# One fused attention, gated-convolution and mixer kernel: weights decoded two tiles to an operation, pooled scores by head, a new order of work

## The chip, the cores and the metric

The kernel runs on one core of one Trainium2 chip. The metric is the device time of one execution in microseconds (us). The engines are named as the profile names them: PE (TensorE) multiplies and PEld loads its weights, DVE is VectorE, ACT is ScalarE, POOL is GpSimd, SP issues the transfers.

## The reference

Three blocks follow one another. Sizes: batch 4, 8 heads, 576 positions, head width 64, so 4 x 576 tokens of 512 channels.

```python
# 1: attention, scale 1/8, factor 4
q_d, k_d, v_d = (t.reshape(B, H, 144, 4, 64).mean(axis=3) for t in (q, k, v))
out = np.repeat(softmax(scale * q_d @ k_d.T) @ v_d, 4, axis=2)          # pooled
out += softmax(where(abs(i - j) < 4, scale * q @ k.T, -1e9)) @ v        # local
x = out.transpose(0, 2, 1, 3).reshape(B, 576, 512)
# 2: gated convolution, w_in 512 x 1024, three taps over the positions, w_out 1024 x 512
h = relu(x @ w_in)
x = (h * sigmoid(conv(h, conv_w))) @ w_out
# 3: low-rank mixing of the positions (rank 32), then a channel product, 512 -> 2048 -> 512
u = x + (x.T @ U @ V).T
out = u + relu(u @ w_ch1) @ w_ch2
```

Inputs q, k and v are 32-bit; the weights of blocks 2 and 3 are 64-bit numbers and reach the chip as pairs of 32-bit words.

## The kernel before

**Attention** works on 16 pairs (two heads of one batch on 128 partitions). Pair p needs three loads: `lq` (q and k, 576 KB), `lw` (values for the local part, 384 KB), `lr` (values for the pooled part, 288 KB). `qs` sums q and k over four positions (`sums`, L355); `qd` copies the summed q of both heads into a zeroed block matrix (`q_blocks`, L374). `S`, `Sd` are the local and pooled scores on PE, `M`, `Md` the maxima, `D` subtracts them on DVE (`dp` does it on PE), `E`, `Ed` are the exponentials on ACT, `R`, `re`, `r` row sums and reciprocals, `n`, `nd` the normalisation, `T`, `Td` transposes, `c`, `cd` copies out of PSUM, `V`, `Vd` products with the values, `xd`, `x` the sum into the tile `X`, which holds two batches. `vs` sums the pooled values. A suffix says the engine: `nv`, `ndv`, `vsv`, `cv`, `cdv`, `xdv`, `wO`, `gL`, `pL`, `mL`, `sA`, `sl`, `bl` run on DVE; `n`, `nd`, `vs`, `wo`, `gl`, `pl`, `ml`, `sa`, `sL`, `bL` on POOL; `c`, `cd`, `xd` on ACT. `f.n` puts n matmuls into PE's queue whose results nobody uses.

**Weights** come in tiles of 128 x 512 64-bit words (512 KB by the profile). `wl` loads a tile; `wd` decodes it to a 32-bit number: step 0 on ACT (L583), steps 1 to 3 on DVE (L585, L587, L590). `wh` copies the rounded upper part on ACT (L603), `wo` or `wO` takes the remainder on POOL or DVE (L606). Every product of blocks 2 and 3 is made of three matmuls, high x high, high x low, low x high. Decoded values wait in three buffers `wval` of one tile each. There are 16 such tiles for block 2 and 32 for block 3.

**Block 2** runs over 6 token blocks of 384 and, in each, over 8 blocks f of 128 hidden channels; n = 8 * block + f. `1.n.cc` is the first product (L719), `r1` the relu, `c0` and `c1` the taps, `th` tanh, `gt`/`gm` the gate, `gh` and `gl`/`gL` its upper part and remainder, `2.n.c` the second product (L773). Token block 0 needs pairs 0 to 3 in `X`, token block 1 (from `1.8.0` on) pairs 4 to 7 too, and with block 0 all 16 tiles have been needed.

**Block 3**: `mh`, `mi`, `mo`, `ma` mix; then the channel product by a scheme with 7 instead of 8 half products (`p`, L925; second product `4`, L957). Its left operands `as` are made from decoded tiles (`sa`, `sh`, `sl`), written to HBM (`sw`) and read again twice (`sr`) into 10 buffers.

**Order**: nothing is reordered by a compiler. The string `SEQ` is a list of some 2,900 words; each word calls one function, and each engine executes its instructions in the order of the list. An instruction waits for its data and for its buffer, and what stands behind it on its engine waits with it. All loads are issued by SP in the order of the list; `load` makes the 44 first ones also wait for an earlier load, so that about 900 KB are under way.

Of the kernel before, what the change touches and what calls it, by code (L numbers as in the profile page):

```python
# [1064 lines left out]
```

## Time and profile before

| | us |
|---|---|
| runs | 725.91, 726.84, 728.79 (median 726.84) |
| the profiled execution's own time | 723.91 |
| its span, first to last instruction | 722.1 |
| busy in the span: PE, DVE, ACT, POOL | 696.3, 463.2, 354.7, 186.0 |
| mean granted PE clock | 0.988 of full |

Busy PE includes matmuls that overlap: the group of L957 shows 216.9 us for 864 matmuls of 393 ns each, so two lie over one another most of the time. Shares over the span mix stages with different limits; the text that follows goes by stages.

### The profile page before, as it was taken

Reading aid. Unit: us, or ns where it says so; the run is one execution under the profiler, and the core shown is the slowest. Engines: PE = TensorE matmul, PEld = TensorE weight load, DVE = VectorE, ACT = ScalarE, POOL = GpSimd, SP = SyncE. Lnnn points to the kernel's source line nnn. Section 1 sums busy time; section 2 is a strip of 40 time slices with the busy share of each in tenths; the row PEclk is TensorE's granted clock in tenths of the full one; section 3 lists DMA queues with packets and bytes.
Section 4 is the critical chain, followed back from the end, with each engine's and each line's share of the span. In section 5 each row is a group of like instructions: output and inputs, shape, how many; then the busy total and the mean of one; then the engine's idle time right before and its main releaser. Section 6 shows DMA issues by size and latency. Waiting matters only on the chain.

```text
span 722.1 us, 14566 instructions
## 1 busy us (share of the span) xinstructions
PE 696.3 (96%) x5785; PEld 615.8 (85%) x5785; DVE 463.2 (64%) x807; ACT 354.7 (49%) x818; POOL 186.0 (26%) x186
## 2 busy tenths in 40 slices
...
GB/s 265 285 303 246 179 99 24 73 73 75 61 2 1 1 1 30 87 162 134 302 170 237 226 244 228 159 182 119 129 118 117 96 101 199 117 131 118 114 45 88
DMA packets 40580, 96.43 MB, mean 134 GB/s; under 512 B 4672, under 2 KB 5184, under 8 KB 40512
## 3 DMA queue, kind: packets, MB, share of 16 engines
...
q8 instruction: 46, 0.75, 0.4%
...
## 4 chain that ended last, share of the span: by engine, by line
PE 82%; DVE 9%; DMA 3%; issue 2%; ACT 2%; POOL 1%; SPq 0%; DVEq 0%; ACTq 0%; POOLq 0%
PE acc L957 25%; PE g L925 23%; PE g L719 13%; PE acc L773 12%; DVE wval L590 1%; DMA vr<-in_vr_dram 1%; PE O L528 1%; DVE wval L587 1%; PE h L797 1%; PE S L394 1%; PE Sd L460 1%; PE O L536 1%; DVE vb L893 1%; DVE wval L585 1%; DMA vw<-in_vw_dram 1%
## 5 line engine op out<-in xcount | busy, mean ns | idle before, releaser
L957 PE MATMUL acc<-w,a 128*128 128x512 f32 x864 | 216.9, 393 | 0.0
L925 PE MATMUL g<-bt,as 128*128 128x384 f32 x1008 | 194.3, 338 | 1.0 <-ACT tp L930 0.6
L925 PEld LDWEIGHTS g<-bt,as 128*128 128x128 f32 x1008 | 178.7, 188 | 11.5 <-ACT tp L930 1.0
L957 PEld LDWEIGHTS acc<-w,a 128*128 128x128 f32 x864 | 159.9, 188 | 26.4
L719 PE MATMUL g<-xhl,w 128*128 128x386 f32 (+1 forms) x576 | 114.4, 343 | 0.0
L773 PE MATMUL acc<-w,ghl 128*128 128x512 f32 x432 | 110.0, 395 | 0.2 <-DVE ghl L765 0.2
L719 PEld LDWEIGHTS g<-xhl,w 128*128 128x128 f32 x576 | 101.4, 189 | 4.2 <-issue 0.8
L934 DVE TENSOR_TENSOR tp<-g,tp 128x384 f32<-128x384 f32 x72 | 39.9, 555 | 93.3 <-ACT tp L930 51.0
L773 PEld LDWEIGHTS acc<-w,ghl 128*128 128x128 f32 x432 | 79.6, 188 | 15.5 <-issue 0.8
L930 ACT ACTIVATE tp<-g 128x384 f32<-128x384 f32 x72 | 35.2, 488 | 103.5 <-PE g L925 101.4
L945 DVE SCALAR_TENSOR_TENSOR a<-tp,a 128x384 fp32r<-128x384 f32 x72 | 41.6, 578 | 68.0 <-ACT a L941 67.8
L746 DVE SCALAR_TENSOR_TENSOR g<-h,cw,g 128x384 f32<-128x384 f32 x96 | 59.2, 617 | 24.5 <-ACT g L741 23.1
L941 ACT ACTIVATE a<-tp 128x384 fp32r<-128x384 f32 x72 | 37.7, 525 | 74.7 <-PE acc L957 53.9
L765 POOL TENSOR_TENSOR ghl<-ct,ghl 128x384 fp32r<-128x384 f32 x40 | 42.1, 1052 | 119.9 <-ACT ghl L762 116.0
L914 POOL TENSOR_TENSOR bt<-vb,bt 128x384 fp32r<-128x384 f32 x16 | 16.7, 1060 | 142.8 <-ACT bt L910 142.7
L606 POOL TENSOR_TENSOR w<-wval,w 128x512 fp32r<-128x512 f32 x20 | 26.8, 1343 | 52.8 <-ACT w L603 51.3
L587 DVE SCALAR_TENSOR_TENSOR wval<-raw,wval 128x512 uint32<-128x512 uint32 x48 | 38.2, 796 | 1.2
L590 DVE SCALAR_TENSOR_TENSOR wval<-raw,wval 128x512 uint32<-128x512 uint32 x48 | 37.5, 786 | 0.8
L725 ACT ACTIVATE h<-g 128x386 f32<-128x386 f32 (+1 forms) x48 | 23.6, 491 | 23.4 <-PE g L719 23.2
L583 ACT ACTIVATE wval<-raw 128x512 f32<-128x512 f32 x48 | 31.4, 667 | 4.3 <-POOL w L606 1.5
L941 ACT ACTIVATE a<-g 128x384 fp32r<-128x384 f32 x24 | 11.8, 491 | 40.8 <-PE acc L957 33.3
L762 ACT ACTIVATE ghl<-ct 128x384 fp32r<-128x384 f32 x40 | 20.9, 523 | 20.5 <-PE acc L773 14.5
...
## 6 DMA issues: line engine op xcount, KB each, us to landing
as<-s SPq DMA_DIRECT2D x112, 256.0 KB, 2.8
...
s<-as SPq DMA_DIRECT2D x56, 256.0 KB, 4.0
...
out_dram<-u SPq DMA_DIRECT2D x17, 256.0 KB, 3.2
...
```

The source lines that it names most:

```text
L587: eng.scalar_tensor_tensor(out=d, in0=lo, scalar=29, in1=d, op0=ALU.logical_shift_right, op1=ALU.bitwise_or)
L590: eng.scalar_tensor_tensor(out=d, in0=hi, scalar=0x80000000, in1=d, op0=ALU.bitwise_and, op1=ALU.bitwise_or)
L719: nc.tensor.matmul(gp[n][:, :wd], w[:, a, cc], xhl[g, cc][:, b, :wd], start=cc == 0 and i == 0, stop=cc == NCC - 1 and i == 2)
L746: nc.vector.scalar_tensor_tensor(out=o, in0=inner(g, hts[n], k), scalar=cw[:, k * NF + f:k * NF + f + 1], in1=o, op0=ALU.mult, op1=ALU.add)
L765: eng.tensor_tensor(ghl[n][:, 1], cts.pop(n), ghl[n][:, 0].bitcast(F32), op=ALU.subtract)
L773: nc.tensor.matmul(acc[g][c], t[:, a, c * P:(c + 1) * P], w[:, b], start=f == 0 and i == 0, stop=f == NF - 1 and i == 2)
L925: nc.tensor.matmul(o, w[:, a, k], Bs[r, j, k][:, b, :TB], start=j in (0, 1, 3) and n == 0, stop=n == 3 * HC - 1, skip_group_check=True)
L930: nc.scalar.activation(out=t[:, :TB], in_=bank[q, 0][:, :TB], func=AF.Copy)
L934: nc.vector.tensor_tensor(t, bank[q, 1][:, :TB], t, op=ALU.add)
L941: nc.scalar.activation(out=t[:, 0], in_=r_src(q, k), func=AF.Relu)
L945: nc.vector.scalar_tensor_tensor(out=t[:, 1], in0=r_src(q, k), scalar=0.0, in1=t[:, 0].bitcast(F32), op0=ALU.max, op1=ALU.subtract)
L957: nc.tensor.matmul(acc2[g][c], t[:, a, c * P:(c + 1) * P], w[:, b], start=f == 0 and n < 2 and i == 0, stop=f == NFP - 1 and n >= 2 and i ...
```

## The change

1. **Weights by pairs.** Two tiles share one buffer, one decoded value of 128 x 1024 and one `wd`, `wh` sequence: steps 0 to 3 and `wh` are one instruction for two tiles. Loads and remainders stay one tile each. `wval` has two buffers of two tiles instead of three of one.
2. **Pooled scores by head.** `q_blocks` and its zeroed tiles go. The scores of one block of 48 positions are two matmuls, one a head, each with 64 rows and 64 columns (16 of them unused), at the same time on 128 partitions. The scale moves into the exponential and into a small new operation on the maxima (`ns` on ACT or `nS` on DVE). The softmax works on 128 instead of 96 partitions; the transposes `Td` move 128 instead of 96 columns.
3. **First load in halves.** `lq.0` loads half the positions and `lh.1` the other; `qs.0` and `qt.1` sum one half each. The two casts `K` move from DVE to ACT. `rE` adds the epsilon on DVE (`re` does it on ACT).
4. **The list** is another one for attention and block 2, and again for block 3. Ten buffers `as` become nine. The function of the local product, `pv_local`, is the same in both.

```diff
-    KPB, NAS = 3, 10
+    KPB, NAS = 3, 9
-    pv = ctx.enter_context(tc.tile_pool(name="pv", bufs=3, side="right", reuse_waits="tile"))
+    pv = ctx.enter_context(tc.tile_pool(name="pv", bufs=2, side="right", reuse_waits="tile"))
-        nc.vector.tensor_copy(identR, ident)
-        nc.vector.tensor_copy(mask, maskf)
+        nc.scalar.activation(out=identR, in_=ident, func=AF.Copy)
+        nc.scalar.activation(out=mask, in_=maskf, func=AF.Copy)
...
         for j in range(3):
-            nc.tensor.matmul(s[:, j], e["qd"][:, j], e["ss"][:, 1], start=True, stop=True)
+            for h in range(2):
+                rows = slice(D * h, D * h + D)
+                nc.tensor.matmul(s[rows, j], ss[rows, 48 * j:48 * j + D], ss[rows, SD:], start=True, stop=True)
...
+    def scale_d(p, eng):
+        t = st[p]["nm"][:, 12:]
+        if eng == "ACT":
+            nc.scalar.activation(out=t, in_=t, func=AF.Copy, scale=SCALE / 16)
+        else:
+            nc.vector.tensor_scalar(out=t, in0=t, scalar1=SCALE / 16, scalar2=None, op0=ALU.mult)
...
-                nc.tensor.transpose(s[:72, c, 96 * j:96 * j + 96], e["Pd"][:, j, 72 * c:72 * c + 72], ident[:96, :96])
+                nc.tensor.transpose(s[:72, c, P * j:P * j + P], e["Pd"][:, j, 72 * c:72 * c + 72], ident)
...
+    def w_load(k, j, h):
+        if h == 0:
+            t = wp.tile([P, 2, 512 * Z], U32 if Z == 2 else F32, name="raw", tag=f"w{j if k == 1 else j // 2}")
+            raws[k, j] = t.rearrange("p i (n z) -> p (i n) z", z=Z)
...
+    def w_dec(k, j, step):
         if step == 0:
-            vals[k] = pv.tile([P, 512], F32, name="wval", tag="wval")
-        dec(raws[k], vals[k], step, eng)
+            vals[k, j] = pv.tile([P, 1024], F32, name="wval", tag="wval")
+        dec(raws[k, j], vals[k, j], step)
...
+    def w_hi(k, j):
+        W[k, j] = wp.tile([P, 2, 2, 512], F32R, name="w", tag=f"w{j if k == 1 else j // 2}")
+        nc.scalar.activation(out=W[k, j][:, :, 0], in_=vals[k, j].rearrange("p (i n) -> p i n", i=2), func=AF.Copy)
+    def w_lo(eng, k, j, h):
+        eng.tensor_tensor(W[k, j][:, h, 1], vals[k, j][:, 512 * h:512 * h + 512], W[k, j][:, h, 0].bitcast(F32), op=ALU.subtract)
```

The list before, up to the first products of block 2:

```
sf xz lq.0 z k uz wm lr.0 sp.1 lw.0 lq.1 sp.0 qs.0 sp.1 lq.2 K qd.0 vs.0.0 S.0.2 lr.1 lw.1 vs.0.1 Sd.0.1 M.0 f.1 dp.0
Md.0 lq.3 E.0 qs.1 f.3 S.1.1 Ed.0 R.0 qd.1 M.1 re.0 f.3 Sd.1.1 lr.2 r.0 D.1 nd.0 wl.1.0 qs.2 E.1 n.0 lq.4 vs.1.0 R.1
qd.2 f.8 T.0.0 Md.1 Td.0.2 c.0 vsv.1.1 S.2.1 Ed.1 qs.3 lr.3 lw.2 vs.2.0 cd.0 re.1 qd.3 r.1 lc ndv.1 V.0.2 wl.1.1 n.1
wd.1.0.0 M.2 wd.1.0.1 wd.1.0.2 Vd.0 wd.1.0.3 wl.1.2 wh.1.0 Sd.2.1 vsv.3.0 xd.0 vs.2.1 x.0 lq.5 dp.2 cw.0 wO.1.0 px.0.0
cw.1 pL.0.0 lr.4 T.1.0 E.2 cw.2 lw.3 Md.2 Td.1.2 wd.1.1.0 cw.3 R.2 Ed.2 S.3.1 wl.1.3 wd.1.1.1 wd.1.1.2 wd.1.2.0
wd.1.1.3 re.2 c.1 wd.1.2.1 wd.1.2.2 Sd.3.1 wh.1.1 wd.1.2.3 lq.6 wo.1.1 r.2 wh.1.2 V.1.0 cdv.1 wl.1.4 nv.2 wo.1.2 M.3
D.3 T.2.0 lw.4 vsv.4.0 E.3 Vd.1 nd.2 c.2 Md.3 R.3 wd.1.3.0 Td.2.2 vs.3.1 xdv.1 wl.1.5 Ed.3 x.1 V.2.1 wd.1.3.1 cd.2
wd.1.3.2 wl.1.6 px.0.1 wd.1.3.3 re.3 pl.0.1 Vd.2 qs.4 wd.1.4.0 lr.5 wh.1.3 wl.1.7 S.4.0 wd.1.4.1 qd.4 wo.1.3 r.3 qs.5
xd.2 lw.5 n.3 wd.1.5.0 x.2 qd.5 wd.1.4.2 Sd.4.0 px.0.2 wd.1.4.3 wd.1.6.0 lq.7 pl.0.2 M.4 wh.1.4 T.3.1 D.4 wo.1.4 c.3
Md.4 f.2 S.5.0 wl.1.8 qs.6 E.4 vs.5.0 wd.1.7.0 wl.1.9 R.4 Ed.4 wd.1.6.1 V.3.2 wd.1.6.2 qd.6 wd.1.7.1 lq.8 re.4
wd.1.7.2 wd.1.5.1 wd.1.5.2 lw.6 wd.1.5.3 ndv.3 wh.1.5 r.4 f.10 Td.3.1 wo.1.5 wl.1.10 M.5 Sd.5.0 cd.3 D.5 wd.1.7.3
wd.1.8.0 Vd.3 n.4 Md.5 wh.1.7 wl.1.11 wd.1.8.1 xd.3 wo.1.7 E.5 qs.7 Ed.5 nd.4 x.3 qd.7 f.14 T.4.0 S.6.0 wd.1.8.2 %Z
px.0.3 vsv.4.1 pL.0.3 lr.6 1.0.0 vs.5.1 lq.9 M.6 1.0.1 wd.1.8.3 1.0.2 lr.7 1.0.3 wd.1.6.3 wh.1.8 1.1.0
```

The list after, up to the same word:

```
sf z k lq.0 uz wm lh.1 sp.1 xz lq.1 sp.0 lc K qs.0 lr.0 sp.1 lq.2 qt.1 S.0.2 lr.1 qs.1 cw.0 S.1.1 wl.1.0.0 cw.1 vs.0.0
M.0 Sd.0.1 D.0 vs.0.1 M.1 E.0 Sd.1.0 lw.0 cw.2 cw.3 Md.0 R.0 ns.0 lq.3 Ed.0 dp.1 vsv.1.0 Md.1 vs.1.1 E.1 lq.4 rE.0
ns.1 r.0 Ed.1 qs.2 nd.0 lw.1 n.0 R.1 f.6 T.0.1 rE.1 r.1 ndv.1 wl.1.0.1 Td.0.2 c.0 qs.3 S.2.1 cd.0 lr.2 nv.1 Sd.2.1 M.2
T.1.0 lr.3 qs.4 S.3.2 wl.1.1.0 Td.1.0 cv.1 wd.1.0.0 dp.2 M.3 Sd.3.0 E.2 Md.2 lq.5 vs.2.0 R.2 ns.2 V.0.1 Ed.2 Md.3
wl.1.1.1 vsv.3.0 re.2 dp.3 nS.3 wd.1.0.1 Ed.3 Vd.0 wl.1.2.0 wd.1.0.2 cd.1 vs.2.1 E.3 r.2 f.7 V.1.0 wl.1.2.1 qs.5 xd.0
nd.2 Vd.1 n.2 R.3 lq.6 wd.1.1.0 rE.3 r.3 f.3 T.2.1 wd.1.0.3 Td.2.2 xd.1 lr.4 Sd.4.0 n.3 cd.2 x.0 wh.1.0 wd.1.1.1
wl.1.3.0 wd.1.1.2 px.0.0 pl.0.0 x.1 lw.2 vsv.3.1 px.0.1 f.14 S.4.0 wo.1.0.0 cv.2 wl.1.3.1 qs.6 T.3.1 vs.4.0 c.3 lw.3
M.4 wo.1.0.1 Md.4 f.4 dp.4 lw.4 V.2.2 E.4 lq.7 wd.1.1.3 wd.1.2.0 Vd.2 pl.0.1 R.4 S.5.0 wh.1.1 wd.1.2.1 lr.5 vs.4.1
ns.4 V.3.1 Ed.4 M.5 wO.1.1.1 wl.1.4.0 re.4 wO.1.1.0 xd.2 wd.1.2.2 wd.1.3.0 wl.1.4.1 wd.1.2.3 lq.8 vs.5.0 r.4 wh.1.2
x.2 wl.1.5.0 ndv.3 px.0.2 wo.1.2.0 D.5 f.14 Td.3.2 E.5 wl.1.5.1 wO.1.2.1 pl.0.2 Sd.5.0 R.5 wd.1.4.0 wd.1.3.1 lw.5 cd.3
n.4 Md.5 f.5 Vd.3 wd.1.3.2 ns.5 Ed.5 wl.1.6.0 nd.4 qs.7 xd.3 f.5 T.4.0 re.5 S.6.0 vs.5.1 wl.1.6.1 c.4 x.3 lw.6
wd.1.4.1 px.0.3 %Z f.1 1.0.0 pl.0.3 1.0.1 M.6 1.0.2 r.5 lr.6 wd.1.3.3 1.0.3 lr.7 dp.6 r1.0 n.5 1.1.0
```

Words that stand in the two lists ahead of `1.0.0` and of `1.8.0` (a `wd` or `wh` of the new list covers two tiles):

```
word            before 1.0.0   before 1.8.0
                was  becomes   was  becomes
wd step 0         9    5         16    8
wd steps 1-3     25   12         48   24
wh                7    3         16    8
wO                1    3          2    6
wo                6    3         13   10
qs                8    8         11   12
qt                0    1          0    1
qd                8    0         11    0
ns                0    5          0    7
nS                0    1          0    2
M                 6    6         10    9
Md                6    6         10    9
D                 4    2          7    3
dp                2    4          3    6
R                 5    6          9    9
r                 5    5          8    9
re                5    3          8    6
rE                0    3          0    3
nv                1    1          1    2
n                 4    4          7    7
ndv               2    2          2    2
nd                3    3          6    7
vsv               4    3          7    3
vs                7    9         14   17
c                 4    3          6    6
cv                0    2          2    2
cd                3    4          7    8
cdv               1    0          1    0
x                 4    4          8    7
xd                3    4          5    6
xdv               1    0          3    1
K                 1    1          1    1
gt                0    0          7    0
gm                0    0          0    7
gL                0    0          7    0
gl                0    0          0    6
pL                2    0          2    2
pl                2    3          6    5
S                 7    7         10    9
Sd                6    6         10   10
T                 5    5          8    8
Td                4    4          8    8
V                 4    4          8    7
Vd                4    4          8    7
f (matmuls)      41   59         48   59
2                 0    0         16   18
```

## Rows read from the trace of the kernel before

**Rows 1.** Stretches: us, busy PE, PEld, DVE, ACT, POOL, PEclk, DMA share, GB/s
```profile
0.00:58.00 58.00, 43.45 (x1043) 34.39 (x1043) 48.96 (x80) 34.26 (x100) 27.37 (x35) 0.85 0.86 283
58.00:98.00 40.00, 35.87 (x494) 30.41 (x486) 38.14 (x65) 29.69 (x71) 22.68 (x20) 1.00 0.54 177
98.00:323.00 225.00, 224.68 (x2295) 200.64 (x2294) 167.09 (x293) 144.86 (x338) 80.00 (x75) 1.00 0.16 52
323.00:718.00 395.00, 392.27 (x1965) 350.36 (x1963) 208.19 (x370) 145.84 (x310) 55.97 (x57) 1.00 0.47 152
```

**Rows 2.** What DVE waited for, 58 to 98 us: total, times, longest
```profile
DVE X L555 <- PE O L330: 1.0, 1, 1.0
DVE wval L585 <- ACT wval L583: 0.2, 1, 0.2
```

**Rows 3.** Groups of DVE instructions by line and form, whole span
```profile
L587 DVE SCALAR_TENSOR_TENSOR wval<-raw,wval 128x512 uint32<-128x512 uint32 x48 | 38.2, 796 | 1.2
L590 DVE SCALAR_TENSOR_TENSOR wval<-raw,wval 128x512 uint32<-128x512 uint32 x48 | 37.5, 786 | 0.8
L585 DVE TENSOR_SCALAR wval<-wval 128x512 uint32<-128x512 uint32 x48 | 24.8, 516 | 1.0 <-ACT wval L583 0.8
...
L465 DVE TENSOR_REDUCE nm<-Sd 96x3 f32<-96x432 f32 x16 | 9.5, 595 | 0.4 <-PE Sd L460 0.3
...
L606 DVE TENSOR_TENSOR w<-wval,w 128x512 fp32r<-128x512 f32 x12 | 8.6, 716 | 0.4 <-ACT w L603 0.3
...
L416 DVE TENSOR_TENSOR P<-S,nm 128x384 f32<-128x384 f32 x13 | 7.2, 553 | 0.7 <-PE S L330 0.4
...
L765 DVE TENSOR_TENSOR ghl<-g,ghl 128x384 fp32r<-128x384 f32 x8 | 4.4, 544 | 0.4 <-ACT ghl L762 0.3
...
L585 DVE TENSOR_SCALAR cw<-cw 128x24 uint32<-128x24 uint32 x1 | 0.2, 170 | 0.0
```

**Rows 4.** Timeline, DVE and POOL: start, duration, engine, line
```profile
21.24 0.69 DVE L587 SCALAR_TENSOR_TENSOR wval<-raw,wval 128x512 uint32<-128x512 uint32 x1
...
29.66 1.26 POOL L606 TENSOR_TENSOR w<-wval,w 128x512 fp32r<-128x512 f32 x1 [8.74 <-ACT w L603]
29.72 1.75 DVE L590 SCALAR_TENSOR_TENSOR wval<-raw,wval 128x512 uint32<-128x512 uint32 x1
...
81.32 2.71 POOL L606 TENSOR_TENSOR w<-wval,w 128x512 fp32r<-128x512 f32 x2
```

**Rows 5.** ACT's first decode step, groups by line, 0 to 98 us
```profile
L583 ACT ACTIVATE wval<-raw 128x512 f32<-128x512 f32 x16 | 10.7, 676 | 3.5 <-POOL w L606 1.5 <-POOL P L453 1.4 <-DMA raw<-in_w_dram 0.4
```

**Rows 6.** Timeline, PE
```profile
58.01 2.21 PE L719 MATMUL g<-xhl,w 128*128 128x386 f32 x11
...
85.13 0.92 PE L528 MATMUL O<-PT,vw 64*64 64x48 f32 x48
85.97 0.72 PE L536 MATMUL O<-PTd,vd 72*64 72x144 f32 x8
...
104.47 0.90 PE L460 MATMUL Sd<-ss,qd 128*96 128x144 f32 x6
105.11 0.46 PE L387 MATMUL S<-mask,identR 128*128 128x192 f32 x2
...
106.44 0.97 PE L773 MATMUL acc<-w,ghl 128*128 128x512 f32 x3
...
110.06 1.76 PE L719 MATMUL g<-xhl,w 128*128 128x388 f32 x9
...
115.62 0.49 PE L494 MATMUL T<-front,P 128*128 128x128 f32 x3
115.95 0.66 PE L501 MATMUL Td<-front,Pd 96*72 96x96 f32 x6
116.39 1.32 PE L719 MATMUL g<-xhl,w 128*128 128x388 f32 x6
```

**Rows 7.** Transfers of block 3's left operands: count, KB each, us to landing
```profile
as<-s SPq DMA_DIRECT2D x112, 256.0 KB, 2.8
```

More of the change, by code (lines that the diff above doesn't have):

```diff
@@ L277, in mixer_kernel @@
     eps = const.tile([P, 2], F32, name="eps")
-    qds = [pa.tile([P, 3, 96], F32, name=f"qd{i}") for i in range(2)]
     sms = [pa.tile([P, 15], F32, name=f"sm{i}") for i in range(3)]
@@ L299, in clear @@
             nc.gpsimd.memset(t, 1.0)
-        for t in qds:
-            nc.gpsimd.memset(t, 0.0)
     def warm():
@@ L321, in slot_a @@
         t = last["a"] = (ps0 if n < 1 else pst).tile([P, 2, 512], F32, name=name, tag=f"a{n}")
+        last["w"] = 64 if name == "Td" else 112
         last["sum"] = name == "S" and f"dp.{p}" in words_
@@ L327, in beat @@
     def beat(n, start=False):
-        for _ in range(n):
-            nc.tensor.matmul(last["a"][:, 1, 288:512], identR, mask[:, :112].unsqueeze(1).to_broadcast([P, 2, 112]), start=start or not last["sum"], stop=True, skip_group_check=True)
+        w = last["w"]
+        for _ in range(n if w > 64 else 2 * n):
+            nc.tensor.matmul(last["a"][:, 1, 512 - 2 * w:], identR, mask[:, :w].unsqueeze(1).to_broadcast([P, 2, w]), start=start or not last["sum"], stop=True, skip_group_check=True)
     def dense(n):
-        for _ in range(n):
-            nc.tensor.matmul(last["a"][:, 1, 288:512], ident, ident[:, :112].unsqueeze(1).to_broadcast([P, 2, 112]), start=not last["sum"], stop=True, skip_group_check=True)
+        w = last["w"]
+        for _ in range(n if w > 64 else 2 * n):
+            nc.tensor.matmul(last["a"][:, 1, 512 - 2 * w:], ident, ident[:, :w].unsqueeze(1).to_broadcast([P, 2, w]), start=not last["sum"], stop=True, skip_group_check=True)
     def slot_b(n, name):
@@ L340, in load_qk, with load_half @@
         t = (xu if p % 3 == 2 else pa).tile([P, 2, S], F32, name="qk", tag=("qk0", "qk1", "xu3")[p % 3])
-        load(t, qk[p], 576)
         st[p]["qk"] = t
+        if p == 0:
+            load_half(0)
+        else:
+            load(t, qk[p], 576)
+    def load_half(h):
+        cols = slice(S // 2 * h, S // 2 * h + S // 2)
+        load(st[0]["qk"][:, :, cols], qk[0][:, :, cols], 288)
     def load_vw(p):
@@ L353, in sums, with sums_half @@
         e = st[p]
-        t = e["ss"] = pa.tile([P, 2, SD], F32, name="ss", tag="ss", bufs=2)
-        nc.vector.tensor_reduce(out=t.rearrange("p z x -> p (z x)"),
-                                in_=e["qk"].rearrange("p z (x t) -> p (z x) t", t=4), op=ALU.add, axis=AX.X)
+        e["ss"] = pa.tile([P, 2, SD], F32, name="ss", tag="ss", bufs=2)
+        if p == 0:
+            sums_half(0)
+        else:
+            nc.vector.tensor_reduce(out=e["ss"].rearrange("p z x -> p (z x)"),
+                                    in_=e["qk"].rearrange("p z (x t) -> p (z x) t", t=4), op=ALU.add, axis=AX.X)
+    def sums_half(h):
+        e = st[0]
+        nc.vector.tensor_reduce(out=e["ss"][:, :, SD // 2 * h:SD // 2 * h + SD // 2],
+                                in_=e["qk"][:, :, S // 2 * h:S // 2 * h + S // 2].rearrange("p z (x t) -> p z x t", t=4),
+                                op=ALU.add, axis=AX.X)
     def sums_pe(p, n):
@@ L366, in sums_copy @@
         t = e["ss"] = pa.tile([P, 2, SD], F32, name="ss", tag="ss", bufs=2)
-        nc.scalar.activation(out=t[:, 1], in_=e["sq"][:, 1], func=AF.Copy)
-    def q_blocks(p):
-        e = st[p]
-        e["qd"] = qds[p % 2]
-        for h in range(2):
-            rows = slice(D * h, D * h + D)
-            nc.scalar.activation(out=e["qd"][rows, :, 48 * h:48 * h + 48],
-                                 in_=e.get("sq", e["ss"])[rows, 0].rearrange("p (j r) -> p j r", j=3), func=AF.Copy, scale=SCALE / 16)
+        nc.scalar.activation(out=t, in_=e.pop("sq"), func=AF.Copy)
     WS = [min(max(0, NQ * i - 4), S - NW) for i in range(S // NQ)]
@@ L487, in vsum, with vsum_pe, vsum_copy, eps_dve @@
             eng.tensor_tensor(d.rearrange("p h c d -> p (h c d)"), t[:, 0], t[:, 1], op=ALU.add)
+    def vsum_pe(p, n):
+        e = st[p]
+        t = e["vq"] = slot_b(n, "vq")[:72, :4 * D]
+        r = e["vr"].rearrange("p t h c d -> p t (h c d)")
+        for i in range(4):
+            nc.tensor.matmul(t, ident[:72, :72], r[:, i], start=i == 0, stop=i == 3)
+    def vsum_copy(p):
+        e = st[p]
+        d = e["vd"] = pa.tile([72, 2, 2, D], F32, name="vd", tag="vd", bufs=2)
+        nc.scalar.activation(out=d.rearrange("p h c d -> p (h c d)"), in_=e.pop("vq"), func=AF.Copy)
+    def eps_dve(p):
+        t = st[p]["sm"]
+        nc.vector.tensor_scalar(out=t, in0=t, scalar1=1e-9, scalar2=None, op0=ALU.add)
     def trans(p, n):
```

60 lines of the change are left out of this document (24 added, 36 removed), and 378 rows, old and new, of the table SEQ.

## The prediction

> **What bounds the kernel now.** I read the views from the coarse to the fine: stretches, waits, groups, timeline.
>
> The stretches [rows 1] split the run in two. From 98 us to the end of the products PE is busy 224.68 of 225 us and 392.27 of 395. What is listed there is PE's own work, and an edit that takes time from another engine gains nothing. Before 98 us it is otherwise: DVE is busy 48.96 us of the first 58 (it has no data at first) and 38.14 of the next 40, while PE has gaps. From 58 to 98 us DVE waits for others only 1.0 + 0.2 us [rows 2]. So PE waits there for a chain that runs through DVE, and DVE waits for nobody: it is the bound, and its queue sets when block 2 reaches full speed.
>
> Two words serve as marks: `1.0.0`, the first product of block 2, which starts at 58.01 us, and `1.8.0`, the first that needs pairs 4 to 7, at 110.06 us [rows 6]. The reader is to see that PE's time behind `1.8.0` does not depend on the path to it. The question is how much earlier the new list arrives there, and how much PE work it has left then.
>
> **DVE's work ahead of the marks.** I count the words of the two lists (the table in the section on the change) and multiply by the mean of each word's group; the large terms are in [rows 3], and small ones by the same view. The old list has 51.9 us of DVE work ahead of `1.0.0`, reached at 58.0, and 104.8 ahead of `1.8.0`, reached at 110.1. Both lie 5 to 6 us under the clock, which is about what DVE loses at the start. So the sum tracks the time, though as a list sum: some of what is listed ahead is done a little later.
>
> The terms that differ ahead of `1.8.0`:
> - Decoding. An operation on 24 elements takes 0.170 us (the last of [rows 3]), which is the fixed part; a double one costs twice the single minus that: 2 x 0.796 - 0.17 = 1.42, 2 x 0.786 - 0.17 = 1.40, 2 x 0.516 - 0.17 = 0.86 us. Eight pairs by three steps save 24 x 0.17 = 4.1 us. Bounds: nothing saved, if two tiles cost twice one, and 9.2 us, if the slower-than-alone part of the means goes too (one such step alone takes 0.69 instead of 0.796 us [rows 3, 4]; 48 x 0.106 = 5.1). I take 4.1.
> - Seven remainders `gL` go to POOL: 7 x 0.544 = -3.8. Four remainders `wO` come from POOL: 4 x 0.716 = +2.9.
> - Four subtractions `D` become matmuls on PE: 4 x 0.553 = -2.2.
> - Four fewer `vsv` (-1.8); the casts `K`, two `xdv` and one `cdv` (-1.8) leave DVE.
> - One pair less is begun ahead of the mark: `M`, `Md` (0.595) and `x`, together -1.9.
> - More: one `qs` and the halves of the first (+1.4), one `nv` (+0.55), `nS`, `rE` and one `r` (+1.1).
>
> The sum is -9.7: 95.1 instead of 104.8. By the same count 48.8 instead of 51.9 stand ahead of `1.0.0`, so it should start at 54.9, and `1.8.0` at 100.4.
>
> [...]
>
> **PE's work behind the mark.** The new list has one `S`, `V` and `Vd` less ahead of `1.8.0` and two words `2` more. `S` takes 106.44 - 105.11 = 1.33 us, `V` 85.97 - 85.13 = 0.84, `Vd` at most 0.72 [rows 6]; a word `2` is three matmuls of 512 columns, 3 x 216.9 / 864 = 0.75 us by the group quoted under the table. So 1.33 + 0.84 + 0.72 - 1.5 = +1.4 us are left over.
>
> `Td`: six transposes of 96 columns take 116.39 - 115.95 = 0.44 us, 0.073 each; three of 128 columns in `T` take 0.33, 0.11 each [rows 6]. The new ones have 128 columns but 72 weight columns, as now: between 0.073 and 0.11. By columns 0.098, +0.15 us a pair. Eight (`Td.8` to `Td.15`) lie behind the mark: +1.2, bounds 0 and +1.8.
>
> `Sd`: now 105.11 - 104.47 = 0.64 us. The trace has no matmuls in its new shape, but `V` has 64 x 64 ones on both halves: 48 instructions of 48 columns in 0.84 us. At that rate 12 of 144 columns take 0.84 x 1728 / 2304 = 0.63 us, the same. I take 0. If the two heads do not run side by side it is 1.26, +0.63 for each of the six behind the mark.
>
> **Edits at nothing.** The extra idle matmuls `f` and the three `dp` ahead of `1.8.0` lie in gaps of PE (14.6 us of the first 58 [rows 1]); without these gaps up to 22 matmuls of 224 columns, 0.11 us each by the columns of the group quoted under the table, would cost 2.4, and three `dp` less than three `S`, 4.0. ACT loses work (`qd`, half the decoding and `wh`) and was busy 34.26 of 58 us; uncovered, nothing. The first load: two small transfers now go ahead of a half, so the first sum starts about when it did; bounds -1 and +1. Block 3: PE covers DVE (208.19 of 395 us) and POOL; with one of its buffers `as` gone an operand may be fetched two instead of three operands ahead of a set of seven. A set lasts 395 / 24 = 16.5 us, an operand 2.4, so 4.7 us lead remain over the 2.8 us of a landing [rows 7]. If transfers took longer than that, each set would wait for the excess.
>
> **The sum.** 9.7 - 1.4 - 1.2 = 7.1 us less. The profiled execution's own 723.91 becomes 716.8; its span 722.1 becomes 715.0. The median of the runs shown is 726.84, 2.9 above that execution; the same 7.1 gives 719.7. About 0.5%, 3.6 us, is what a measurement can tell from no change.
>
> **Rivals.**
> - *DVE gives it back to POOL.* At 29.66 us POOL begins an operation of 1.26 us, and DVE's step beside it takes 1.75 instead of 0.69 [rows 4]: it ends 0.55 us after POOL does. The new list has more POOL work ahead of `1.8.0`: six `gl`, one `nd`, three `vs` more, three `wo` and one `pl` less, +4.9 us. If DVE stands still for all of it, 2.2 us remain: 724.6. Against it: the means that I multiplied hold such waits already, and DVE sheds two-input work too. [...]
> - *Loads become the bound.* By the sizes of the loads 16,217 KB (16.6 MB) stand ahead of `1.0.0` now, which at 283 GB/s [rows 1] is 58.7 us, and 16,953 KB (17.4 MB) in the new list: 61.3 us. If `1.0.0` waits for all of them it starts 3.3 us later than now instead of 3.1 earlier, and 0.7 us of gain remain: 726.1. Against it: what `1.0.0` needs ends with `lw.3` after 11,289 KB, at 41 us, and DVE did not wait for loads after the start.
> - *The heads do not overlap in `Sd`.* 6 x 0.63 = 3.8 less: 723.5.
> - *Two tiles cost twice one.* 4.1 less: 723.8.
> - *ACT waits for the two `wval` buffers, and it is slower.* Step 0 of pair j + 2 waits on ACT until the remainders of pair j are taken, and the relus, exponentials and taps queue behind it. Now ACT lost 1.5 us to POOL's remainders in 98 us [rows 5]. Two remainders on POOL last 2.71 us [rows 4]; if each of six such waits (pairs 2 to 7) costs PE that, 16.3 us go against 7.1: 736.0. It decides from 1.2 us a wait on. Against it: every remainder of pair j stands ahead of that step in the new list, with at least three words between.
>
> **How the numbers follow.** Forecast 0.66; POOL 0.08, loads 0.09, heads 0.05, decoding 0.04, slower 0.08. The likeliest gives 719.7 us. The range goes up to the loads' case, 726.0, beyond which lies the slower one; down to the upper bound of the decoding, 7.1 + 5.1 = 12.2 less, 714.6. Faster by over 0.5%: the forecast and a part of the cases at 3.3 to 3.0 us, 0.70. Within 0.5%: 0.20. Slower: 0.10.
>
> **What would show it.** Right: the first product of block 2 near 55 us and the first of token block 1 near 100; double decoding steps of 1.4 and 0.86 us; DVE still above 90% busy between them; PE gapless from some 90 us on; `Td` near 0.6 us, `Sd` near 0.64. Wrong: DVE idle behind loads or behind ACT in that stretch, double steps of 1.6 us, POOL's operations beside DVE steps of over 2 us, or gaps of PE after 323 us in front of `as`.

## The result and the profile after

The changed kernel takes 733.3 us (median of 7 runs), the one before 727.71 (7 runs): a ratio of 1.0083, 95% interval 1.0057 to 1.0109, so slower by 0.8%, where 719.7 us and 1% faster were forecast. The profiled execution of after took 729.87 us (span 728.1), 6.0 more than that of before; the clock was 0.990 of full.

The stretches of [rows 1], after (columns as there):

```profile
0.00:58.00 58.00, 45.52 (x1000) 36.01 (x1000) 43.01 (x64) 26.74 (x69) 24.17 (x30) 0.89 0.89 286
58.00:98.00 40.00, 39.02 (x605) 34.33 (x605) 37.13 (x50) 30.55 (x72) 32.29 (x27) 0.99 0.47 153
98.00:323.00 225.00, 224.62 (x2359) 196.50 (x2345) 159.90 (x273) 134.66 (x311) 89.56 (x86) 1.00 0.14 45
```

DVE is idle for 15.0 us of the first 58, not 9.0, though it has less to do. The first product of block 2 (`1.0.0`) starts at 63.41 us; before it was 58.01, forecast 54.9. The group of DVE's double steps that answers to [rows 3]:

```profile
L615 DVE SCALAR_TENSOR_TENSOR wval<-raw,wval 128x1024 uint32<-128x1024 uint32 x24 | 33.2, 1385 | 0.3
L612 DVE SCALAR_TENSOR_TENSOR wval<-raw,wval 128x1024 uint32<-128x1024 uint32 x24 | 32.9, 1370 | 0.3
L610 DVE TENSOR_SCALAR wval<-wval 128x1024 uint32<-128x1024 uint32 x24 | 19.5, 812 | 3.2 <-ACT wval L608 3.2
```

1.37, 1.39 and 0.81 us, where 1.42, 1.40 and 0.86 were worked out. So the operations cost what I said, and the opening came out late all the same. What DVE, then PE, waited for ahead of 63.4 us (total, times, longest):

```profile
DVE ss L362 <- DMA qk<-in_qk_dram: 4.4, 2, 3.4
DVE nm L409 <- PE S L394: 3.2, 2, 2.0
DVE ss L357 <- DMA qk<-in_qk_dram: 1.9, 1, 1.9
PE T L520 <- POOL P L453: 2.7, 2, 2.5
PE Td L527 <- DVE Pd L487: 2.6, 1, 2.6
PE Sd L463 <- issue: 2.2, 2, 1.6
PE S L394 <- issue: 1.9, 1, 1.9
```

How one such wait travels, in the timeline of PE and DVE:

```profile
47.63 0.75 PE L394 MATMUL S<-qk 64*24 64x32 f32 x62 [1.92 <-issue]
...
48.41 0.56 DVE L409 TENSOR_REDUCE nm<-S 128x12 f32<-128x384 f32 x1 [1.98 <-PE S L394]
48.89 2.36 DVE L628 TENSOR_TENSOR w<-wval,w 128x512 fp32r<-128x512 f32 x2
51.17 1.21 DVE L612 SCALAR_TENSOR_TENSOR wval<-raw,wval 128x1024 uint32<-128x1024 uint32 x1
52.41 1.23 DVE L615 SCALAR_TENSOR_TENSOR wval<-raw,wval 128x1024 uint32<-128x1024 uint32 x1
...
54.33 0.60 DVE L487 TENSOR_TENSOR Pd<-Pd,sm 128x432 f32<-128x432 f32 x1
...
55.07 1.47 PE L527 MATMUL Td<-front,Pd 128*72 128x128 f32 x6 [2.63 <-DVE Pd L487]
...
63.41 2.29 PE L741 MATMUL g<-xhl,w 128*128 128x386 f32 x12
```

PE stands still in the middle of `S.5`; DVE, in order, waits for those scores; two remainders and two double steps stand ahead of the normalisation `ndv.3`; PE then waits for that. The granted clock is 0.81 of full from 50 to 63.4 us: 0.50 from 48.5 to 51.5 and from 55.07 to 58.0 us, behind the 1.92 and the 2.63 us for which PE had stood idle, and 1.00 from 58.5 us on. The six transposes take 1.47 us here at 0.50, and 0.82 at 67.77 us.

Three stretches tell the kernels apart: the first product; from the first relu of block 2 to the first of token block 1; from there to the last relu of block 2.

| kernel | ratio to before, 95% | first product, us | to token block 1 | to the last relu |
|---|---|---|---|---|
| before | 1 | 58.0 | 53.9 | 208.7 |
| after | 1.0083, 1.0057 to 1.0109 | 63.4 | 52.8 | 208.4 |
| e5_pooled_alone | 1.0059, 1.0036 to 1.0081 | 59.6 | 55.5 | 211.1 |
| e7_sd_by_v | 1.0174, 1.0135 to 1.0214 | 68.2 | 59.4 | 208.1 |
| e2_nofill | 1.0052, 1.0029 to 1.0076 | 64.7 | 52.8 | 208.3 |
| e8_head | 1.0084, 1.0053 to 1.0115 | 69.1 | 53.0 | 208.7 |
| e3_single | 1.0214, 1.0194 to 1.0234 | 67.5 | 58.8 | 208.6 |
| e4_whole | 1.0044, 1.0021 to 1.0066 | 64.3 | 53.0 | 208.3 |
| e12_whole_nofill | 1.0004, 0.9986 to 1.0021 | 61.3 | 53.0 | 208.3 |
| e13_oldpool | 1.0097, 1.0071 to 1.0123 | 70.3 | 55.5 | 206.1 |
| e14_all | 1.0050, 1.0033 to 1.0066 | 60.8 | 56.6 | 206.2 |
| e15_fewer_loads | 1.0018, 0.9995 to 1.0042 | 61.1 | 53.0 | 208.3 |
| e16_no_dp | 0.9998, 0.9972 to 1.0023 | 60.0 | 52.8 | 208.4 |
| e17_order | 1.0053, 1.0032 to 1.0074 | 62.0 | 52.9 | 208.3 |
| e18_order_no_dp | 1.0017, 0.9992 to 1.0041 | 61.0 | 52.9 | 208.3 |
| e19_order2 | 1.0041, 1.0022 to 1.0060 | 61.1 | 53.1 | 208.8 |
| e20_order2_f | 1.0056, 1.0032 to 1.0079 | 62.8 | 52.8 | 208.7 |
| e21_order3 | 1.0022, 1.0001 to 1.0044 | 57.0 | 54.4 | 208.3 |

The times in us are of one profiled execution each, the ratios of all runs (one of the 12 runs of e2 took 3821 us and is not counted). One execution says little of the first product: e7 has the words of after, in their order, up to there, and 68.2 instead of 63.4 us. The two later stretches repeat within 0.6 us where the words in them are the same.

So executions differ ahead of the first relu. From it to the end of the span the kernels with the words of after behind it (after, e2, e4, e8, e12, e15 to e20) take 662.2 to 663.0 us, before 661.7. The median run less this stretch, and less the 1.8 us by which a run is longer than its span, gives an estimate of the first relu in a usual run: 69.2 us in after, 64.0 in e12 and 63.8 to 64.2 in before. The profiled execution of before, with its first relu at 60.4 us, was a quick one.

### The profile page after: what moved, and what is told of

Same layout as the page of the kernel before. It is cut to its first block, busy times and chain, and to the rows that moved or that the text cites. A ratio compares the mean times of both kernels' runs of the same rounds, so it can differ in the third digit from the quotient of the medians.

```text
span 728.1 us, 14685 instructions
## 1 busy us (share of the span) xinstructions
PE 708.3 (97%) x5931; PEld 622.0 (85%) x5931; DVE 450.1 (62%) x722; ACT 343.0 (47%) x748; POOL 216.4 (30%) x207
## 4 chain that ended last, share of the span: by engine, by line
PE 91%; DVE 4%; DMA 2%; issue 1%; ACT 1%; POOL 0%; SPq 0%; DVEq 0%; ACTq 0%; POOLq 0%
PE acc L981 27%; PE g L949 25%; PE g L741 14%; PE acc L795 13%; PE S L394 2%; PE Sd L463 1%; PE O L555 1%; PE Td L527 1%; PE h L819 1%; DMA vr<-in_vr_dram 1%; PE O L563 1%; PE g L902 1%; PE T L520 1%; PE mx L840 1%; DVE w L628 1%
## 5 line engine op out<-in xcount | busy, mean ns | idle before, releaser
L981 PE MATMUL acc<-w,a 128*128 128x512 f32 x864 | 219.7, 393 | 0.0
L969 DVE SCALAR_TENSOR_TENSOR a<-tp,a 128x384 fp32r<-128x384 f32 x72 | 43.3, 603 | 53.9 <-ACT a L965 52.9
L787 POOL TENSOR_TENSOR ghl<-ct,ghl 128x384 fp32r<-128x384 f32 x48 | 51.0, 1064 | 85.2 <-ACT ghl L784 79.7
L628 POOL TENSOR_TENSOR w<-wval,w 128x512 fp32r<-128x512 f32 x18 | 29.7, 1659 | 29.6 <-ACT w L625 29.6
L784 ACT ACTIVATE ghl<-ct 128x384 fp32r<-128x384 f32 x48 | 25.0, 523 | 20.5 <-PE acc L795 10.6
L779 DVE SCALAR_TENSOR_TENSOR ct<-g,h 128x384 f32<-128x384 f32 x48 | 26.5, 552 | 12.3 <-POOL ghl L787 8.2
L615 DVE SCALAR_TENSOR_TENSOR wval<-raw,wval 128x1024 uint32<-128x1024 uint32 x24 | 33.2, 1385 | 0.3
L612 DVE SCALAR_TENSOR_TENSOR wval<-raw,wval 128x1024 uint32<-128x1024 uint32 x24 | 32.9, 1370 | 0.3
```

The lines of the kernel that those rows point to most:

```text
L615: nc.vector.scalar_tensor_tensor(out=d, in0=hi, scalar=0x80000000, in1=d, op0=ALU.bitwise_and, op1=ALU.bitwise_or)
L628: eng.tensor_tensor(W[k, j][:, h, 1], vals[k, j][:, 512 * h:512 * h + 512], W[k, j][:, h, 0].bitcast(F32), op=ALU.subtract)
L787: eng.tensor_tensor(ghl[n][:, 1], cts.pop(n), ghl[n][:, 0].bitcast(F32), op=ALU.subtract)
L969: nc.vector.scalar_tensor_tensor(out=t[:, 1], in0=r_src(q, k), scalar=0.0, in1=t[:, 0].bitcast(F32), op0=ALU.max, op1=ALU.subtract)
L981: nc.tensor.matmul(acc2[g][c], t[:, a, c * P:(c + 1) * P], w[:, b], start=f == 0 and n < 2 and i == 0, stop=f == NFP - 1 and n >= 2 and i ...
```

## The experiments

Theory A: the tile shapes of the new pooled scores cost PE time. Theory B: the opening is late, through PE's queue and its idle matmuls (B1) or DVE's waits (B2). Theory C: the double operations and their two buffers make others wait. Theory D: they save DVE's time, as forecast.

**Pooled scores alone (e5_pooled_alone),** on the kernel before:

```diff
-            nc.tensor.matmul(s[:, j], e["qd"][:, j], e["ss"][:, 1], start=True, stop=True)
+            for h in range(2):
+                rows = slice(D * h, D * h + D)
+                nc.tensor.matmul(s[rows, j], ss[rows, 48 * j:48 * j + D], ss[rows, SD:], start=True, stop=True)
```

> The kernel before with the pooled scores of 64 rows a head alone: Sd as 12 matmuls of 64 x 64, the scaling of nm behind each Md, Td with 128 columns; the order of the work, the decoding and the first load stay as before. Theory A (the tile shapes on PE cost the loss): in the trace of the changed kernel Td's slot grew from 0.44 to 0.57 us and Sd's from 0.64 to 0.88, and the 0.2 us of idle time that PE's weight loads show at a change between 128-row and 64-row tiles comes twice more for each pair. That is about 0.55 us for each of some ten pairs in the stretch where PE has no gaps: 5 to 6 us more than the kernel before, a ratio near 1.0075, with the first product of block 2 near 58 us as before. Theory C (the decoding of two tiles to an operation with its two buffers costs the loss): no difference from before, a ratio within 0.002 of 1.

0.59%, 4.3 us: theory A for this part. 2.4 us of it fall behind token block 1, where PE has no gaps. There PE's weight loads (PEld), first of before, then of after:

```profile
104.24 0.89 PEld L460 LDWEIGHTS Sd<-ss,qd 128*96 128x96 f32 x6
105.09 0.31 PEld L387 LDWEIGHTS S<-mask,identR 128*128 128x128 f32 x2
```

```profile
107.40 1.00 PEld L741 LDWEIGHTS g<-xhl,w 128*128 128x128 f32 x6
108.65 0.68 PEld L463 LDWEIGHTS Sd<-ss 64*64 64x64 f32 x12 [0.26 <-ACT PTd L544]
109.53 1.01 PEld L741 LDWEIGHTS g<-xhl,w 128*128 128x128 f32 x6 [0.20 <-issue]
```

`Sd` held PE from 104.24 to 105.09, 0.85 us; now it is 1.13, from the end of the loads before (108.40) to 109.53, with idle time on both sides at the change of tile shape, 0.26 and 0.20 us. The release by ACT named there is no cause: at 159.59 us the same place shows 0.25 us put down to "issue". 6 x 0.28 = 1.7, and 8 `Td` of 0.57 instead of 0.44 us (from the start of the six transposes to that of the next group) another 1.0: 2.7, where the stretch shows 2.4. How much of the 0.28 us is the change of shape was not measured by itself.

**`Sd` next to `V` (e7_sd_by_v):** words moved, six like this.

```diff
- Sd.12.0 c1.16.2 px.3.1 cdv.10 1.17.0 th.16 pl.3.1 1.17.1 gm.16 V.10.0
+ c1.16.2 px.3.1 cdv.10 1.17.0 th.16 pl.3.1 1.17.1 gm.16 Sd.12.0 V.10.0
```

> The changed kernel with six of the Sd words put directly ahead of a V, so that two groups of 64 x 64 tiles stand side by side and one pair of shape changes is saved at each place; what follows from Sd moves behind V. Theory A: 6 x 0.4 = 2.4 us less than the changed kernel's 733.3, so about 730.9 and a ratio to before of 1.005; at each such place no 0.2 us of idle weight loads between Sd and V. If the shape changes cost nothing: the ratio stays at 1.008.

A miss: 1.0174, 0.9% over the changed kernel. Three of the six words stand ahead of token block 1, and that stretch takes 59.4 instead of 52.8 us; behind it the other three won 0.2 us, not 1.2, though no idle weight load stands there between `Sd` and `V`. So this run does not bear out a price of 0.4 us for a pair of shape changes. In its opening an operation of 0.60 us took 5.45. DVE, then POOL:

```profile
51.05 5.45 DVE L477 TENSOR_TENSOR Pd<-Pd,sm 128x432 f32<-128x432 f32 x1
```

```profile
50.94 1.26 POOL L484 TENSOR_TENSOR vr<-vr 72x512 f32<-72x512 f32 x1 [4.85 <-DMA vr<-in_vr_dram]
52.17 1.26 POOL L618 TENSOR_TENSOR w<-wval,w 128x512 fp32r<-128x512 f32 x1
53.39 0.99 POOL L720 TENSOR_TENSOR xhl<-X,xhl 128x386 fp32r<-128x386 f32 x1
54.34 0.83 POOL L443 TENSOR_TENSOR P<-P,sm 128x384 f32<-128x384 f32 x1
55.13 0.90 POOL L477 TENSOR_TENSOR Pd<-Pd,sm 128x432 f32<-128x432 f32 x1
```

POOL had waited for a load with four operations queued behind it, ran all five without a break, and DVE's operation, begun 0.11 us after the first of them, ended after the last.

**No extra idle matmuls (e2_nofill):** all nine words `f.n` removed.

> The changed kernel without its nine words of extra idle matmuls f (59 of them ahead of the first product of block 2, which I had costed at nothing). Theory B1 (PE reaches the first product of block 2 late because idle matmuls stand in its queue when the data are there, and because its instruction stream stalls, 1.6, 0.7 and 1.9 us in the trace of after): the stalls shrink, the first product comes 2 to 4 us earlier than 63.4 us, and the time is 2 to 4 us under 733.3. Theory B2 (DVE with its waits sets the first product, and the idle matmuls only fill PE's gaps and hold the clock up): the first product at 63 us or later, as the matmuls ahead of it run at the lower clock, and the time the same or up to 2 us more.

1.0052 against 1.0083: 0.31%, 2.3 us, which is no more than the two intervals leave open (e12 repeats it below). The size is B1's, the profile is not: its stalls were not shorter (3.7 and 1.7 us), its first product not earlier. The granted clock ahead of it is 0.76 without them and 0.89 with them, so the time fell at a lower clock. Only 18 of the 59 matmuls are the change's: the kernel before has 41 in the same stretch, and it was not run without them.

**Maxima ahead of the second load (e8_head):**

```diff
- qs.1 cw.0 S.1.1 wl.1.0.0 cw.1 vs.0.0 M.0 Sd.0.1 D.0
+ M.0 D.0 qs.1 cw.0 S.1.1 wl.1.0.0 cw.1 vs.0.0 Sd.0.1
```

> The changed kernel with M.0 and D.0 put ahead of qs.1, so that DVE takes the maxima of the first pair while the second pair's load is still under way (in the trace of after DVE waits 1.86 us for that load with the first scores ready). Theory B2 (DVE's sum plus its waits set the first product of block 2): it comes 1 to 2 us earlier than 63.4 us, and the time falls by as much, a ratio to before near 1.006. Theory B1 (PE's queue and its stalls): the first product stays at 63 us.

No change in the time. DVE's wait for the second pair's load fell from 1.9 to 0.3 us, and its waits for `S` rose from 3.2 to 5.5.

**Order of before (e10_old_pairs, e9_old_list):** pairs decoded where their first tile was. In both, two sums of block 3 (`sA.5.0`, `sA.7.0`) are formed before an operand's last decoding step.

> The kernel before (its order of the work, its pooled scores with qd, its first load whole) with the decoding of two tiles to an operation alone; a pair is decoded where the first of its tiles was, both raw tiles are loaded there, and one buffer PT less makes the room. Theory D (the step of the prediction that I still hold: a double operation saves one fixed part, 24 x 0.17 us of DVE's time ahead of token block 1, and DVE is the bound there): the first product of token block 1 comes 3 to 4 us earlier than in the kernel before, and the ratio is near 0.995. Theory C (the longer operations and the two buffers make PE wait): no gain, a ratio of 1.000 or more.

> The code of the changed kernel (pooled scores of 64 rows a head, two tiles to an operation), but in the order of the work of the kernel before and with the first load and sum whole. Against the changed kernel it shows what the searched order is worth, against the run with the pooled scores alone (ratio 1.006) what the double operations are. Theory D: 0.995 + 0.006, a ratio near 1.001, as the order and not the parts made the first product of block 2 late. Theory C: 1.008 or more.

1.0544 (1.0520 to 1.0567) and 1.0633 (1.0606 to 1.0659). First products at 63.1 and 67.5 us, 59.8 and 58.7 us from there to token block 1: placed by so plain a rule, the double operations make the opening later than single ones did, against the forecast of theory D. Three quarters of the loss (32 of 44 us in e10) come after the 40th relu, where my placing moved work of blocks 2 and 3 too, so the ratios of these two say little on theory D.

**One instruction for each tile (e3_single):**

```diff
-        dec(raws[k, j], vals[k, j], step)
+        for h in range(2):
+            dec(raws[k, j][:, 512 * h:512 * h + 512], vals[k, j][:, 512 * h:512 * h + 512], step)
```

> The changed kernel in which each decoding step and each leading half wh is again one instruction for each tile, at the same places, with the buffers of the changed kernel. Theory D: 24 fixed parts of 0.17 us come back on DVE ahead of token block 1, and the time is 3 to 4 us above 733.3, a ratio near 1.013. Theory C, in the form that the long operations keep other work of DVE and ACT waiting: the same or faster than 733.3.

1.0214: 1.3%, 9.5 us over the changed kernel; 6.1 of them between first relu and token block 1, 2.1 behind it. Theory D holds in this list, which was made for double operations. The single steps take 0.81, 0.84 and 0.56 us here, two of each 0.84 us a pair more than the double ones: 6.7 us of DVE for eight pairs, where 4.1 were forecast and 9.2 the bound. The rest of the 9.5 isn't told apart, as ACT's step 0 and `wh` are single again too. Theory C falls in this form.

**First load whole (e4_whole):** `lh.1` and `qt.1` removed.

> The changed kernel with the first load and the first sum whole again. My prediction's bounds for the halves were 1 us either way, so a ratio between 1.007 and 1.010. If the halves are what makes the opening late (DVE waits 1.86 us longer for the second pair's load in the trace of after), 2 us less than 733.3: a ratio near 1.005.

1.0044: 0.39%, 2.8 us won.

**Both undone (e12_whole_nofill).**

> The changed kernel with the first load and sum whole and without the extra idle matmuls f, the two undone together. If they act on different waits of the opening, their gains add: 733.3 - 3.5 - 2.3 = 727.5, a ratio near 1.001. If both take away the same wait (PE late for the chain of the first pairs), the ratio stays at 1.003 to 1.005.

1.0004: the gains add, 0.79% or 5.7 us, and the kernel is level with before. With e2 and e4 this gives each edit twice: the halves cost 2.8 us with the idle matmuls in the list and 3.5 without, the 59 idle matmuls 2.3 us with the halves and 2.9 without.

**Old pooled scores in the new order (e13_oldpool, e14_all).**

> The changed kernel with the pooled scores of the kernel before (qd, three matmuls of 128 x 96 for Sd, Td with 96 columns); to make room vw has two buffers instead of three, and each later load lw stands behind the V that frees its buffer. Theory A (the tile shapes of the new pooled scores cost PE 4.3 us, as in the run with them alone): 4 us less than 733.3, a ratio near 1.003. If in this order of the work they cost nothing, or the later loads cost as much: 1.008 or more.

> All three undone together: first load whole, no extra idle matmuls, pooled scores of the kernel before (two buffers of vw). What stays of the change is the decoding of two tiles to an operation and the searched order. If the three costs add: 733.3 - 3.5 - 2.3 - 4.3 = 723.2, a ratio near 0.995, and faster than both kernels; the gap of 3.6 us to the 719.7 predicted would be what the opening loses besides. If double operations and order gave nothing on their own: a ratio of 1.000 or more.

Both miss the time: 1.0097 for 1.003, 1.0050 for 0.995. Behind token block 1 they win 2.2 us, the size of e5 from the other side; to token block 1 they lose 2.7 to 3.6 (ACT has `qd` again, `vw` one buffer less: not told apart). In this order, and with that buffer given up, going back to the old scores wins nothing.

**Fewer loads (e15_fewer_loads).**

> The changed kernel with the first load whole and without f (ratio 1.000), in which the pairs 3 to 5 are computed from the queries, keys and table vw of the pairs 0 to 2, whose loads are left out: 2.9 MB less of the 17 MB ahead of the first product of block 2. Theory L (the loads fill the DMA engines, over 0.9 of their time from 10 us on, so that DVE waits for qk and vr and PE's instruction stream is fetched late: 3.5 us in one Sd and 1.0 in one S there): the stalls of PE that no engine's work explains shrink to below 1 us each, the first product comes 3 to 5 us earlier than 61.3 us, the ratio is near 0.995. Theory M (the order of the work on DVE and PE alone sets it): the first product stays within 1 us, the ratio at 1.000.

Theory L falls for the time: 1.0018, no gain over e12. PE's timeline in e12, then twice in e15:

```profile
14.26 0.74 PE L447 MATMUL Sd<-ss 64*64 64x144 f32 x4 [3.50 <-issue]
```

```profile
11.52 0.46 PE L455 MATMUL Sd<-ss 64*64 64x144 f32 x4 [0.39 <-issue]
...
47.24 0.34 PE L386 MATMUL S<-qk 64*24 64x32 f32 x14 [1.48 <-issue]
```

The first stop is 3.1 us shorter, and the first product 0.2 us earlier: the transposes `T` behind it wait for POOL's `P`, 5.2 us instead of 1.3, and start at 18.0 us instead of 17.9. That the loads left out shortened the stop isn't shown: with all loads the same stop lasted 0.42 us in e3, 0.65 in e8 and 1.04 in e19, and the later stop in e15, 1.48 us, fell into a stretch with the DMA engines 0.08 busy (0.99 us in e12).

**Subtraction on DVE (e16_no_dp):** `dp.1` to `dp.4` become `D.1` to `D.4`.

> The changed kernel with the first load whole and without f (ratio 1.000), in which the subtraction of the maxima for the pairs 1 to 4 is done by DVE again (D, 0.55 us each) and not by matmuls of PE (dp, 0.82 us each at full clock, and an idle matmul ahead of S). Theory M1 (PE's order in the opening is the longer part, with DVE waiting 5.9 us for S and Sd): the first product of block 2 comes 1 to 2 us earlier, the ratio is near 0.998. My prediction's view (DVE's sum sets it): 4 x 0.55 = 2.2 us later, a ratio near 1.003.

0.9998 against 1.0004: 2.2 us more work for DVE, and the time is not longer, so DVE's sum does not set it. The 1.3 us by which the first product is earlier are less than the 4.8 us between after and e7, whose words are the same up to there.

**Operations moved past decoding (e17, e18, e19, e20, e21);** the core of e21, loads left out:

```diff
- M.5 wO.1.1.1 re.4 wO.1.1.0 xd.2 wd.1.2.2 wd.1.3.0 wd.1.2.3 r.4 wh.1.2 x.2 ndv.3 px.0.2 wo.1.2.0 D.5 Td.3.2 E.5 wO.1.2.1 Sd.5.0 cd.3
+ M.5 wO.1.1.1 re.4 xd.2 x.2 ndv.3 r.4 Td.3.2 wO.1.1.0 cd.3 wd.1.2.2 Sd.5.0 wd.1.3.0 Md.5 ns.5 Ed.5 Vd.3 wd.1.2.3 wh.1.2 px.0.2 n.4
```

> The changed kernel with the first load whole and without f (ratio 1.000), in which four words are moved past decoding work in the opening: the normalisation ndv.3 ahead of the two remainders wO.1.1, the reciprocal r.4 and the sum x.2 ahead of the decoding steps 2 and 3 of pair 2, and n.4 ahead of wo.1.2.0 on POOL. The work is the same. Theory H (operations that are ready stand on DVE behind up to 4.7 us of decoding in longer pieces, and PE waits 3 to 4 us for Pd at some 52 us): the transposes of that Pd start at 48 instead of 52 us, the first product of block 2 2 to 4 us earlier than 61.3, the ratio is 0.995 to 0.998, under both kernels. If DVE's sum sets it (my prediction's view): no change, as the sum is the same.

> The same four moves in the kernel that also has the maxima of the pairs 1 to 4 subtracted by DVE (ratio 1.000 without the moves, first product at 60.0 us). Theory H: first product at 56 to 58 us, a ratio of 0.994 to 0.997. DVE's sum: no change.

> The changed kernel with the first load whole, without f and with the maxima of the pairs 1 to 4 subtracted by DVE (ratio 1.000, first product at 60.0 us), and with six words moved: re.4, xd.2 and x.2 (which frees the PSUM tile that the transposes Td.3 write), ndv.3 and r.4 ahead of the remainder wO.1.1.0 on DVE; cd.3, the copy of these transposes on ACT, ahead of step 0 of pair 4, which waits for a buffer wval; n.4 ahead of wo.1.2.0 on POOL. Theory H2 (the gate was x.2, not the normalisation, and behind it the copy queued on ACT behind a step 0 that waits for the second of two buffers): Td.3 at 49 instead of 52 us, Vd.3 within 3 us of it, the first product at 56 to 57 us, a ratio of 0.995. If the order holds no time: 60 us and 1.000 again.

> The same with the nine words of idle matmuls f kept. If they hold PE's clock up without being waited for, the products of the opening run at the higher clock and the ratio is 0.001 to 0.003 lower than without them; if work waits behind them, as the run without f said (2.3 us), it is 0.003 higher.

> As the run with six words moved (ratio 1.004, Td.3 at 48.5 us as forecast, but its copy on ACT only at 53.5, behind a step 0 that waited 2.6 us for a buffer wval and a wh that waited 1.9 us for DVE), with the rest of that chain moved as well: Td.3 and its copy cd.3 ahead of these two on ACT; Sd.5, its maxima Md.5 and exponentials Ed.5, then Vd.3, xd.3 and x.3 ahead of the later decoding. No work is added or left out. Theory H3 (the opening is a chain of hand-overs between engines, and each that stands behind decoding costs 2 to 4 us): Vd.3 at 51 instead of 54 us, the first product at 56 to 58 us, a ratio of 0.995 to 0.998, under both kernels. If something else sets the first product: 60 to 61 us and a ratio of 1.000 to 1.004.

None is under before. In e17 and e18 `Td.3` waited for `x.2` instead and started at 52.0 and 51.4 us, not at 48. e20, with the nine words `f`, has 1.0056 against 1.0041 without them: less than the noise of the two, so it decides for neither of its two cases. In e19 it started at 48.5 us as forecast, and its copy on ACT stood behind two decoding operations:

```profile
49.11 1.15 ACT L592 ACTIVATE wval<-raw 128x1024 f32<-128x1024 f32 x1 [2.63 <-DVE w L612]
52.14 1.06 ACT L609 ACTIVATE w<-wval 128x1024 fp32r<-128x1024 f32 x1 [1.88 <-DVE wval L599]
...
53.52 0.61 ACT L528 COPY PTd<-Td 72x576 f32<-72x576 f32 x1
```

That is my rival of the two `wval` buffers, at one place. e21 takes it away and has its first product at 57.0 us, as forecast; but later ones of that set wait for `xhl`:

```profile
57.00 2.31 PE L725 MATMUL g<-xhl,w 128*128 128x386 f32 x9
59.84 0.44 PE L725 MATMUL g<-xhl,w 128*128 128x386 f32 x1 [0.53 <-ACT xhl L709]
62.18 0.62 PE L725 MATMUL g<-xhl,w 128*128 128x386 f32 x2 [1.89 <-POOL xhl L714]
```

and the first relu comes at 62.8 us, as in e16 (63.0). In these runs each wait removed was replaced by the next.

## Why the prediction was wrong

- **"So the sum tracks the time" failed.** By the list 48.8 us of DVE's work stand ahead of `1.0.0`, 48.0 were busy in the trace; but the busy time fell by 0.9 us only, not by 3.1, as of the 51.9 us listed before only 49.0 were busy there. And the distance to the clock was not constant: 9.0 us idle became 15.4. DVE was 84% busy in the opening [rows 1], and I took the short waits of 58 to 98 us [rows 2] for the opening too. e16 shows it: more for DVE, no time lost.

```profile
0.00:63.41 63.41, 50.68 (x1132) 40.57 (x1132) 48.04 (x69) 30.32 (x81) 26.50 (x32) 0.89 0.88 283
```

- **"Edits at nothing" failed, and without them the loss is gone.** The first load in halves, bounds 1 us either way, costs 2.8 to 3.5 us. The idle matmuls, nothing as long as PE has gaps, cost 2.3 to 2.9 for all 59; what the 18 added ones cost alone was not run, nor before without its 41, so how the loss of 5.6 us divides between the two edits is open. A gap's length says nothing of when the next data come. That the halves cost because the second pair's load comes later was only argued, and e8 speaks against it.
- **The gain between the marks was more than PE had to give.** I took 6.6 us from DVE there. PE was idle for 4.1 us from `1.0.0` to `1.8.0` before, 0.8 after (the first line is of before):

```profile
58.01:110.06 52.05, 47.92 (x739) 41.28 (x732) 49.41 (x87) 37.97 (x96) 26.16 (x23) 1.00 0.52 170
63.41:110.95 47.54, 46.73 (x605) 40.19 (x604) 44.32 (x62) 34.37 (x79) 37.70 (x30) 1.00 0.39 127
```

The stretch got 4.5 us shorter, but 2.9 of that is one pair's `S`, `V` and `Vd`, which moved behind the mark. From the first relu of block 2 to that of token block 1, where as many of them ran as before, it is 1.2 us (53.94 to 52.75).
- **The work behind the mark was mis-sized.** `1.8.0` started at 110.95 us, where 100.4 was forecast and before had 110.06:

```profile
110.95 1.86 PE L741 MATMUL g<-xhl,w 128*128 128x388 f32 x9
```

617.2 us follow it instead of 612.0, +5.1 for the +2.6 forecast. `Sd`, at nothing, is most of it, 6 x 0.28 = 1.7 us; about 1.0 isn't traced. `V`'s rate gave the matmuls, not the change to their shape, where the trace of after shows 0.26 and 0.20 us of idle weight loads.
- **Right:** the double steps (1.37 for 1.42 us), a gain from them in this list, and `Td` (0.13 for 0.15). Together: `1.0.0` 5.4 us late instead of 3.1 early, 4.5 won to `1.8.0` instead of 6.6, 5.1 given back instead of 2.6: 6.0, by which the two profiled executions differ.
- **Rivals.** A DVE operation that ends only after POOL's beside it (5.45 for 0.60 us in e7) and ACT waiting for a buffer (2.63 us in e19) both occur, at single places. The loss against before is gone without a change to either; whether they hold back the gain that was forecast was tried at a few places only. Loads as the bound fall by e15.
- **Open:** with both edits undone the kernel is level with before, and its first relu in a usual run too (64.0 us against 63.8 to 64.2, the estimate above; the first products of 61.3 and 58.0 us are of one execution each). The 3.1 us forecast for the opening don't appear even so, and the words moved in e17 to e21 won nothing. What holds them back wasn't found.
